# A fused decay-attention and Fourier-mixing kernel: the first batch's decay rates loaded two chunks at a time by token pairs, their running sums as two masked products, and a new stored order

## The chip, the cores and the metric

The kernel runs on one core of a Trainium2 chip. The metric is device time in microseconds (us) of one execution, from start to end, as the median of several runs. A profiled execution gives a trace besides: its span goes from the first to the last instruction. Engines are PE (matmul), ACT (ScalarE), DVE (VectorE), POOL (GpSimd) and SP, which here only issues transfers.

## The reference

Inputs are r, k, v, w of shape (4, 8, 768, 48): batch, head, token, channel. Every head carries a 48 x 48 state that each token's `w` decays:

```
cur   = outer(u * k[t], v[t])
y[t]  = r[t] @ (state + cur)
state = w[t][:, None] * state + outer(k[t], v[t])
```

The heads are then laid side by side, which gives x of shape (4, 768, 384), and a mixing block follows:

```
X   = fft(fft(x, axis=1), axis=2);  u = x + real(X)
un  = (u - mean(u)) / sqrt(var(u) + 1e-6)
out = u + relu(un @ w_ch1) @ w_ch2        # 384 -> 1536 -> 384
```

## The kernel before

**Attention.** The 768 tokens of a batch are six chunks of 128 tokens, one token to a partition; `attention(b, c)` writes the operations of one chunk. A chunk takes four loads (`load_one`, line 619), one each of w, k, r and v: 128 tokens x 8 heads x 48 channels. In memory the 48 fp32 channels of a token and head lie together, so each load moves 1024 runs of 192 B. The decays of a chunk become running sums of logarithms: ACT takes Ln of w into a bf16 buffer `LB` (line 793, shown under line 590, the helper's), and PE multiplies `LB` by a 0/1 mask over tokens, `MSK`, to get the sum over earlier tokens (line 795). A second mask, `NLE`, gives minus the sum up to and with the token itself (line 818, variant `sum_two`); in the variant `sum_add` DVE adds instead (line 832). `total` (lines 803 to 814) gives the sums over the whole chunk by five small products. Exponentials on ACT (lines 822 and 848) turn the sums into factors for r and k; DVE or POOL multiply them in, giving `RH` and `KH` (line 849; line 576, the helper's, `rkh<-in_k,e`). Both are transposed, either on PE with an eviction to `RKT` (lines 890 and 902) or by a transposing DMA from SP (line 880, `rkt<-rkh`). Then come scores (line 913), their masking on DVE (line 923), the state (lines 950 and 958) and the output (lines 975, 978 and 989). In the trace, `rkh` names both halves of one buffer, `ah` the masked scores and `e` the factors.

**Mixing.** `mix(b)` does the Fourier transforms as products with cosine and sine tables (lines 1054 to 1059 and 1098), the statistics (bn_stats, line 1155), the transposes of the normalised rows (on PE, line 1173, or by DMA, line 1180), the first layer (line 1205, with relu evictions at 1211 and 1213) and the second (line 1224, with outputs at 1233 and stores from SP at 1244). Before the first chunk the kernel makes its tables and masks from iotas (POOL, lines 630 to 636) by DVE arithmetic and two sine evaluations on ACT; ACT then loads a second function table (line 705), behind which the first Ln stands.

**What sets the order.** Every operation has a number. `ORDER` holds a list of numbers for each engine, written out by hand or by an earlier search; `schedule` only assigns PSUM banks along it, using estimates of durations. The engines run their lists in order and wait on semaphores. Where the program offers variants (`choose`) or engines, the list says which is used. Thirty-two products of constants (`warm`, line 1291), which nothing reads, and sixteen at the start (line 1257) keep PE occupied; their number is fixed. Input buffers hold seven chunks, `LB` three.

Of the kernel before, what the change touches and what calls it, by code (L numbers as in the profile page):

```python
# [20 lines left out]
PSUM_STATE, NE = 1, 16  # L21
# [44 lines left out]
    "act": (  # L66
# [384 lines left out]
def bass_rwkv6_finch__then__fnet_fourier_mix_kernel(  # L451
# [11 lines left out]
    DM = H * D  # L463
# [861 lines left out]
```

## Time and profile before

| | |
|---|---|
| Three runs, median | 183.09 us (182.51 to 184.56) |
| The profiled execution | 181.76 us |
| Its span, first to last instruction | 179.6 us |
| Around the span | 2.16 us |
| Granted PE clock, mean | 0.999 of full speed |

The profiled execution is 1.33 us below the median. A row of a group gives its busy time and the mean duration of one instruction; PE instructions overlap, so a product's mean duration is longer than the distance from its start to the next one's.

### The profile page before, as it was taken

Reading aid. Unit: us, or ns where it says so; the run is one execution under the profiler, and the core shown is the slowest. Engines: PE = TensorE matmul, PEld = TensorE weight load, DVE = VectorE, ACT = ScalarE, POOL = GpSimd, SP = SyncE. Lnnn points to the kernel's source line nnn. Section 1 sums busy time; section 2 is a strip of 40 time slices with the busy share of each in tenths; the row PEclk is TensorE's granted clock in tenths of the full one; section 3 lists DMA queues with packets and bytes.
Section 4 is the critical chain, followed back from the end, with each engine's and each line's share of the span. In section 5 each row is a group of like instructions: output and inputs, shape, how many; then the busy total and the mean of one; then the engine's idle time right before and its main releaser. Section 6 shows DMA issues by size and latency. Waiting matters only on the chain.

```text
span 179.6 us, 4554 instructions
## 1 busy us (share of the span) xinstructions
PE 172.1 (96%) x1704; PEld 113.7 (63%) x1704; DVE 159.5 (89%) x378; ACT 127.5 (71%) x306; POOL 107.7 (60%) x134
## 2 busy tenths in 40 slices
PE   4989899999999999999999999999989999999994
PEld 2456556766666667777666666766656766655663
DVE  7899899989999899999999999999999997971643
ACT  2899978679996578799999897989960775062200
POOL 2557969496705888499999964997862140500000
PEclk9999999999999999999999999999999999999999
DMA  6999999999999689999997999989972213034033
GB/s 118 217 210 225 183 206 193 203 216 179 162 205 204 145 173 224 199 211 217 202 239 137 224 182 240 235 155 197 245 71 56 74 47 65 1 60 141 0 131 131
DMA packets 117302, 29.28 MB, mean 163 GB/s; under 512 B 112545, under 2 KB 117282, under 8 KB 117282
## 3 DMA queue, kind: packets, MB, share of 16 engines
q1 hardware_dynamic: 115698, 26.65, 72.3%
q0 software_dynamic: 1584, 2.36, 7.9%
q8 instruction: 13, 0.21, 0.5%
q14 instruction: 7, 0.06, 0.1%
HBM read 23.59 MB, written 4.72 MB: 158 GB/s over the span
## 4 chain that ended last, share of the span: by engine, by line
PE 72%; DVE 13%; ACT 7%; POOL 3%; DMA 3%; issue 1%; POOLq 0%; DVEq 0%; ACTq 0%
PE bank L1205 23%; PE bank L1224 23%; PE bank L1098 4%; PE bank L1054 3%; PE bank L913 3%; DMA rkt<-rkh 3%; PE bank L890 2%; PE bank L795 2%; PE bank L978 2%; DVE bst L1155 2%; PE bank L975 1%; DVE uf L1128 1%; ACT rkt L599 1%; PE bank L950 1%; PE bank L818 1%
## 5 line engine op out<-in xcount | busy, mean ns | idle before, releaser
L1224 PE MATMUL bank<-w,ht 128*128 128x384 bf16 (+2 forms) x300 | 53.1, 320 | 0.0
L1205 PE MATMUL bank<-unt,w 128*128 128x384 bf16 x288 | 52.9, 326 | 0.0
L1213 ACT ACTIVATE ht<-bank 128x384 bf16<-128x384 f32 x70 | 31.0, 496 | 21.1 <-PE bank L1205 20.9
L1224 PEld LDWEIGHTS bank<-w,ht 128*128 128x128 bf16 x300 | 27.8, 98 | 15.6
L1205 PEld LDWEIGHTS bank<-unt,w 128*128 128x128 bf16 x288 | 26.6, 98 | 15.8 <-ACT ht L1213 0.2
L923 DVE TENSOR_TENSOR ah<-bank,msk 128x512 bf16<-128x512 f32 x44 | 28.7, 682 | 0.8 <-PE bank L913 0.6
L576 POOL TENSOR_TENSOR rk<-in_r,in_k 128x384 f32<-128x384 f32 x22 | 21.8, 999 | 1.9 <-issue 1.4
L576 POOL TENSOR_TENSOR rkh<-in_k,e 128x384 bf16<-128x384 f32 x18 | 18.0, 1003 | 6.7 <-ACT e L836 4.9
L576 POOL TENSOR_TENSOR rk<-rk,ub 128x384 f32<-128x384 f32 x20 | 19.8, 998 | 3.3 <-DVE rk L576 2.1
L576 POOL TENSOR_TENSOR vtd<-in_v,dc 128x384 f32<-128x384 f32 x20 | 16.4, 829 | 5.1 <-DVE sd L576 1.8
L599 ACT ACTIVATE rkt<-bank 128x512 bf16<-128x512 bf16 (+1 forms) x23 | 16.3, 713 | 4.3 <-PE bank L902 2.8
L1233 DVE SCALAR_TENSOR_TENSOR osb<-bank,rstd,uf 128x384 f32<-128x384 f32 (+2 forms) x24 | 14.3, 594 | 5.5 <-PE bank L1224 3.5
L1211 DVE TENSOR_SCALAR ht<-bank 128x384 bf16<-128x384 f32 x26 | 13.5, 548 | 5.4 <-PE bank L1205 5.2
L863 DVE TENSOR_REDUCE dc<-rk 128x8 f32<-128x384 f32 x24 | 12.7, 544 | 0.4 <-POOL rk L576 0.4
L848 ACT ACTIVATE bank<-bank 128x384 f32<-128x384 f32 x22 | 10.6, 488 | 3.0 <-PE bank L795 2.7
L590 ACT ACTIVATE lb<-in_w 128x384 bf16<-128x384 f32 x24 | 12.6, 528 | 0.1
L590 ACT ACTIVATE un<-uf,agg 128x384 bf16<-128x384 f32 x19 | 11.2, 618 | 1.5 <-DVE agg L1157 0.9
L849 DVE TENSOR_TENSOR rkh<-bank,in_r 128x384 bf16<-128x384 f32 x22 | 11.9, 547 | 0.2 <-ACT bank L848 0.2
L590 ACT ACTIVATE vb<-in_v 128x384 bf16<-128x384 f32 x22 | 11.5, 530 | 0.4 <-DMA in_v<-in_v_dram 0.3
L822 ACT ACTIVATE e<-bank 128x392 f32<-128x392 f32 (+1 forms) x18 | 8.8, 498 | 3.9 <-PE bank L809 2.5
L978 PE MATMUL bank<-vb,ah 128*128 128x48 bf16 x192 | 11.2, 183 | 0.0
L576 POOL TENSOR_TENSOR xf<-sd 128x384 bf16<-128x384 f32 (+1 forms) x7 | 6.9, 1002 | 6.1 <-DVE xf L576 3.9
(178 smaller groups left out, 365.1 us busy)
## 6 DMA issues: line engine op xcount, KB each, us to landing
in_r<-in_r_dram SPq DMA_DIRECT2D x24, 192.0 KB, 3.9
in_k<-in_k_dram SPq DMA_DIRECT2D x24, 192.0 KB, 3.8
in_w<-in_w_dram SPq DMA_DIRECT2D x24, 192.0 KB, 3.8
in_v<-in_v_dram SPq DMA_DIRECT2D x24, 192.0 KB, 3.8
out_dram<-osb SPq DMA_DIRECT2D x23, 192.0 KB, 2.9
w<-in_moe_w_ch_dram POOLq DMA_DIRECT2D x2, 576.0 KB, 7.9
w<-in_moe_w_ch_dram POOLq DMA_DIRECT2D x1, 1152.0 KB, 10.7
out_dram<-osb SPq DMA_DIRECT2D x1, 128.0 KB, 1.8
```

What stands on the lines that cost most here:

```text
L576: return lambda e: e.tensor_tensor(out=o, in0=a, in1=b, op=f)
L590: return lambda e: e.activation(o, a, f, **kw)
L599: {"act": lambda e: e.activation(o(), i(), ACTF.Copy), "dve": lambda e: e.tensor_copy(out=o(), in_=i())}, **kw)
L849: op("dve", v_1(DM), lambda e: e.tensor_tensor(out=rh[:, :, 0:D], in0=ps(tce)[:, 0:DM].rearrange("t (h d) -> t h d", d=D), in1=rt[:, :, :] ...
L863: op("dve", v_1(DM), lambda e: e.tensor_reduce(out=dc[:, :], in_=rku[:, :, :], axis=mybir.AxisListType.X, op=ALU.add), r=[("RK", i2)], w=[ ...
L923: masked[n].append(op("dve", v_1(512), lambda e: e.tensor_tensor(out=ah[:, x:H:2, :], in0=ps(bk)[:, :].rearrange("p (h t) -> p h t", t=128 ...
L978: ins = e.matmul(ps(ty)[:, D * h:D * h + D], ah[:, h, :], vb[:, h, :], start=first and not ype, stop=True, skip_group_check=True)
L1205: ins = e.matmul(ps(t)[:, 0:384], W1[:, m, 256 * (j // 2) + j % 2:256 * (j // 2) + 256:2], unt[:, :, m, :], start=(m == 0), stop=(m == NM ...
L1211: {"dve": lambda e, j=j, t=t, ht=ht: e.tensor_scalar(out=ht[:, j, :], in0=ps(t)[:, 0:384], scalar1=su, scalar2=0.0, op0=ALU.mult, op1=ALU. ...
L1213: "act": lambda e, j=j, t=t, ht=ht: e.activation(ht[:, j, :], ps(t)[:, 0:384], ACTF.Relu, scale=su)},
L1224: ins = e.matmul(ps(t)[:, 0:hi - lo], ht[:, j, 128 * x:128 * x + 128], W2[:, j, lo:hi], start=(j == 0), stop=(j == NJ - 1))
L1233: op("dve", v_1(hi - lo) + 64, lambda e: e.scalar_tensor_tensor(out=o[:, lo:hi], in0=ps(t)[:, 0:hi - lo], scalar=rstd[:, kb:kb + 1], in1=u ...
```

## The change

For batch 0 (`PAIRED = 1`), `load_pair` takes the place of two loads of w: one transfer for two chunks, in which partition p gets tokens 2p and 2p+1 of the 256. For each head the two tokens' channels lie together, so a run is 384 B. Ln runs twice, on the even and on the odd tokens, and the logarithms of a chunk are now spread over both `LB` buffers. Each of the two running sums is thus two accumulated products, with four masks of 128 x 256 (`PM`, in a buffer that the first mixing uses later). The chunk totals take four products more, against two half-indicators `HO` in place of a column of ones. All six chunks of batch 0 use `sum_two`, as they did before. DVE makes the masks and indicators at the start.

Besides this, row blocks of the other batches get a fourth variant (`add_sum`: the mean from an accumulated sum, the variance from an accumulating Square on ACT), four estimates of the scheduler differ, and the whole table `ORDER` is new. Of the table one line of each stands below.

```diff
-PSUM_STATE, NE = 1, 16
+PSUM_STATE, NE, PAIRED = 1, 16, 1
...
-        "7 2354 2355 2356 2357 2358 70 96 98 147 64 149 99 62 150 200 174 119 121 133 201 175 126 143 223 177 "
+        "7 2544 2545 2546 2547 2548 79 103 144 105 146 106 147 71 73 121 122 162 230 163 124 189 190 231 165 "
...
+    INW = sb("in_w", [NIN, H, D], FP32)
+    INB["w"] = [INW[:, i, :, :] for i in range(NIN)]
...
+    PM = UNT[0].rearrange("p a b t -> p (a b t)")[:, 0:1024].rearrange("p (x t) -> p x t", x=4)
...
     def load_one(b, c, n):
+        if n == "w" and b < PAIRED:
+            if c % 2 == 0:
+                load_pair(b, c)
+            return
...
+    def load_pair(b, c):
...
+        loads[b, c, "w"] = loads[b, c + 1, "w"] = op("sp", 750, lambda e: e.dma_start(
+            INW[:, i:i + 2, :, :].rearrange("p a h d -> p (a h d)").rearrange("p (h x) -> p h x", h=H),
+            w[b, :, c * CH:(c + 2) * CH, :].rearrange("h (p a) d -> p h (a d)", a=2)),
...
+        for x, (f0, f1, a1) in enumerate(((ALU.subtract, ALU.is_gt, 0.0), (ALU.subtract, ALU.is_gt, 1.0))):
+            dset(256, ts(PM[:, x, :], CI[:, 128:384], TC[:, 0:1], a1, f0, f1), r=["CI", "TC"], w=[("UNT", 0, x)])
+        dset(256, ts(PM[:, 2, :], CI[:, 128:384], TC[:, 0:1], -1.0, ALU.is_ge, ALU.mult), r=["CI", "TC"], w=[("UNT", 0, 2)])
+        dset(256, ts(PM[:, 3, :], CI[:, 128:384], TC[:, 0:1], -1.0, ALU.is_gt, ALU.mult), r=["CI", "TC"], w=["PM3"])
+        op("dve", 150, fill(PM[0:64, :, 128:256], 0.0), r=[("UNT", 0, 0), ("UNT", 0, 1), ("UNT", 0, 2), "PM3"],
+           w=["PMZ"])
+        op("dve", 60, ts(HO[:, 0, :], TC[:, 0:1].to_broadcast([128, 2]), 63.5, None, ALU.is_lt), r=["TC"], w=["HO0"])
+        op("dve", 60, ts(HO[:, 1, :], TC[:, 0:1].to_broadcast([128, 2]), 63.5, None, ALU.is_gt), r=["TC", "HO0"], w=["HO"])
...
+            def cum(t, m):
+                def f(e):
+                    for x in range(2):
+                        ins = e.matmul(ps(t)[:, 0:DM], PM[:, m + x, 128 * (c % 2):128 * (c % 2) + 128],
+                                       LB[l2[x]][:, :, 0:D], start=x == 0, stop=x == 1)
+                    return ins
...
+                    for x in ([LB[y] for y in l2] if paired else [L]):
+                        ins = e.matmul(ps(t)[:, DM + 2 * h:DM + 2 * h + 2],
+                                       x[:, 2 * h:2 * h + 2, :].rearrange("t h d -> t (h d)"),
+                                       HO[:, c % 2, :] if paired else ONE[:, :], start=False, stop=True,
+                                       skip_group_check=True)
...
+        if paired:
+            sum_two()
+        else:
+            g.choose(("sum", b, c), sum_two, sum_add, sum_key)
...
+                g.choose(("u", b, kb), add_bank, add_row, add_parts, add_sum)
```

Three places show what the new table does. The first is PE's list behind the start-up products, where the sums of chunks 0 and 1 stand; `lb0` and `lb1` are the logarithms, `msk` and `nle` the two masks, `unt0` the buffer that holds the new masks. Before:

```order
L656 MATMUL bank1<-osb0,vtd3 128x384
L795 MATMUL bank2<-lb0,msk 128x384
L818 MATMUL bank3<-lb0,nle 128x384
L795 MATMUL bank4<-lb1,msk 128x384
L749 MATMUL bank5<-ss,unt1 128x193
```

After:

```order
L686 MATMUL bank1<-osb0,vtd3 128x384
L837 MATMUL bank2<-lb0,unt0 128x384
L837 MATMUL bank2<-lb1,unt0 128x384
L837 MATMUL bank3<-lb0,unt0 128x384
L837 MATMUL bank3<-lb1,unt0 128x384
L837 MATMUL bank4<-lb0,unt0 128x384
L837 MATMUL bank4<-lb1,unt0 128x384
L837 MATMUL bank5<-lb0,unt0 128x384
L837 MATMUL bank5<-lb1,unt0 128x384
L856 MATMUL bank4<-pb,idw 128x8
```

Before, three products use one Ln each; after, eight products in a row, of which each bank's second needs the second Ln.

The second place is the head of DVE's list, up to the three instructions `uf<-osb,tc,ht` on which the sines wait. Before:

```order
L587 MEMSET bhpi 128x1
L580 TENSOR_SCALAR tn<-tc 128x3
L581 TENSOR_SCALAR pb<-tc 128x4
L581 TENSOR_SCALAR ht1<-osb2,tn 128x194
L587 MEMSET w1 128x384
L587 MEMSET vtd3 1x128
L587 MEMSET lb0 128x256
L581 TENSOR_SCALAR ht1<-osb2,tn 128x194 x2
L580 TENSOR_SCALAR idw<-osb1 128x384
L581 TENSOR_SCALAR ht1<-ht1 128x582
L584 SCALAR_TENSOR_TENSOR uf1<-osb2,tc,ht1 128x194 x3
```

After:

```order
L588 TENSOR_SCALAR ht1<-osb2,tn 128x194
L594 MEMSET w1 128x384
L588 TENSOR_SCALAR unt0<-osb1,tc 128x256
L588 TENSOR_SCALAR ht1<-osb2,tn 128x194
L594 MEMSET bhpi 128x1
L588 TENSOR_SCALAR ht1<-osb2,tn 128x194
L594 MEMSET rkh2 128x8x8
L588 TENSOR_SCALAR ht1<-ht1 128x582
L594 MEMSET vtd3 1x128
L588 TENSOR_SCALAR nle<-osb1 128x128
L591 SCALAR_TENSOR_TENSOR uf1<-osb2,tc,ht1 128x194
```

The identity (`idw`) has moved behind the three; one of the four new masks (`unt0`), `nle` and small fills have come ahead of them. On POOL the iotas now run in the order token index as integer, `osb1`, `tc`, `osb2`; before, `tc` and `osb2` came first.

The third place is SP's list at the last chunks' transposes, `rkt<-rkh`. Before:

```order
L622 DMA in_v1<-in_v_dram 128x8x48
L1244 DMA out_0_dram<-osb2 128x384
L1244 DMA out_0_dram<-osb0 128x384
L1244 DMA out_0_dram<-osb1 128x384
L880 DMA_TRANSPOSE rkt3<-rkh3 128x8x128
L880 DMA_TRANSPOSE rkt2<-rkh2 128x8x128
```

After:

```order
L633 DMA in_v1<-in_v_dram 128x8x48
L1324 DMA out_0_dram<-osb1 128x384
L633 DMA in_v2<-in_v_dram 128x8x48
L939 DMA_TRANSPOSE rkt2<-rkh2 128x8x128
L939 DMA_TRANSPOSE rkt3<-rkh3 128x8x128
L1324 DMA out_0_dram<-osb0 128x384
```

The three stores that stood right ahead of the two transposes are spread: one stands two places ahead, and one behind them.

More of the change, by code (lines that the diff above doesn't have):

```diff
@@ L299, in schedule @@
                 sw_t = a + o.xfer
+                a -= 200
                 sw.append((a, sw_t))
@@ L484, in bass_rwkv6_finch__then__fnet_fourier_mix_kernel @@
     NT = 4
-    INB = {n: [sb("in_%s%d" % (n, i), [H, D], FP32) for i in range(NIN)] for n in "wkrv"}
+    INW = sb("in_w", [NIN, H, D], FP32)
+    INB = {n: [sb("in_%s%d" % (n, i), [H, D], FP32) for i in range(NIN)] for n in "krv"}
+    INB["w"] = [INW[:, i, :, :] for i in range(NIN)]
     UB = sb("ub", [H, D], FP32)
@@ L508, in bass_rwkv6_finch__then__fnet_fourier_mix_kernel @@
     RSTD = [sb("rstd%d" % i, [NC], FP32) for i in range(2)]
+    MS = [sb("ms%d" % i, [NC, 3], FP32) for i in range(2)]
+    MCO = sb("mco", [2], FP32)
     UN = [sb("un%d" % i, [3, DM], BF16) for i in range(2)]
@@ L623, in load_one @@
                                                 src[n][b, :, c * CH:(c + 1) * CH, :].rearrange("h t d -> t h d")),
-               w=[("in", n, i)], sem="in_%s%d" % (n, i), xfer=985)
+               w=[("in", n, i)], sem="in_%s%d" % (n, i), xfer=998)
         loads[b, c, n] = o
+        g.ctx = was
+    def load_pair(b, c):
+        was, g.ctx = g.ctx, ("load", b, c, "w")
+        i = (b * NC + c) % NIN
+        loads[b, c, "w"] = loads[b, c + 1, "w"] = op("sp", 750, lambda e: e.dma_start(
+            INW[:, i:i + 2, :, :].rearrange("p a h d -> p (a h d)").rearrange("p (h x) -> p h x", h=H),
+            w[b, :, c * CH:(c + 2) * CH, :].rearrange("h (p a) d -> p h (a d)", a=2)),
+            w=[("in", "w", i), ("in", "w", i + 1)], sem="in_w%d" % i, xfer=1400)
         g.ctx = was
@@ L792, in attention @@
         xb = X[b % 2]
-        op("act", a_sb(DM), act(L[:, :, 0:D], wt[:, :, :], ACTF.Ln), r=[("in", "w", i3), "LOGEXP"], w=[("LB", i2)])
         tce = g.tile("a")
-        o = op("pe", mm(DM), lambda e: e.matmul(ps(tce)[:, 0:DM], MSK[:, :], L[:, :, 0:D]),
-               r=["MSK", ("LB", i2)], w=[tce])
+        paired = b < PAIRED
+        if paired:
+            c0 = c - c % 2
+            l2 = [(b * NC + c0 + x) % NB for x in range(2)]
+            if c == c0:
+                wp = INW[:, i3:i3 + 2, :, :].rearrange("p a h d -> p (a h d)").rearrange("p (h a d) -> p h a d", h=H, a=2)
+                for x in range(2):
+                    op("act", a_sb(DM), act(LB[l2[x]][:, :, 0:D], wp[:, :, x, :], ACTF.Ln),
+                       r=[("in", "w", i3), ("in", "w", i3 + 1), "LOGEXP"], w=[("LB", l2[x])])
+            def cum(t, m):
+                def f(e):
+                    for x in range(2):
+                        ins = e.matmul(ps(t)[:, 0:DM], PM[:, m + x, 128 * (c % 2):128 * (c % 2) + 128],
+                                       LB[l2[x]][:, :, 0:D], start=x == 0, stop=x == 1)
+                    return ins
+                return op("pe", mm(DM, 2), f, r=["PMZ", "PM3"] + [("UNT", 0, x) for x in range(3)]
+                          + [("LB", x) for x in l2], w=[t])
+            o = cum(tce, 0)
+        else:
+            op("act", a_sb(DM), act(L[:, :, 0:D], wt[:, :, :], ACTF.Ln), r=[("in", "w", i3), "LOGEXP"], w=[("LB", i2)])
+            o = op("pe", mm(DM), lambda e: e.matmul(ps(tce)[:, 0:DM], MSK[:, :], L[:, :, 0:D]),
+                   r=["MSK", ("LB", i2)], w=[tce])
         if n >= 2:
@@ L808, in tot @@
                 for h in range(HP):
-                    ins = e.matmul(ps(t)[:, DM + 2 * h:DM + 2 * h + 2],
-                                   L[:, 2 * h:2 * h + 2, :].rearrange("t h d -> t (h d)"), ONE[:, :], start=False,
-                                   stop=True, skip_group_check=True)
+                    for x in ([LB[y] for y in l2] if paired else [L]):
[3 more added lines that the diff above has]
+                                       skip_group_check=True)
                 return ins
             if not last:
-                op("pe", mm(1, 5), tot, r=["ONE", "IDB", "PB0", "PB", ("LB", i2)], w=[t])
+                op("pe", mm(1, 9 if paired else 5), tot, r=["HO0", "HO", "IDB", "PB0", "PB"] + [("LB", y) for y in l2]
+                   if paired else ["ONE", "IDB", "PB0", "PB", ("LB", i2)], w=[t])
         def sum_two():
             tci = g.tile("a")
-            op("pe", mm(DM), lambda e: e.matmul(ps(tci)[:, 0:DM], NLE[:, :], L[:, :, 0:D]),
-               r=["NLE", ("LB", i2)], w=[tci])
+            if paired:
+                cum(tci, 2)
+            else:
+                op("pe", mm(DM), lambda e: e.matmul(ps(tci)[:, 0:DM], NLE[:, :], L[:, :, 0:D]),
+                   r=["NLE", ("LB", i2)], w=[tci])
             total(tci)
@@ L844, in sum_key @@
             decays([("E2", i2)])
-        g.choose(("sum", b, c), sum_two, sum_add, sum_key)
+        if paired:
+            sum_two()
+        else:
+            g.choose(("sum", b, c), sum_two, sum_add, sum_key)
         def rh_bank():
@@ L1130, in add_bank @@
                        r=[t, ("X", i, kb)], w=[("UF", i, kb)])
+                    stats()
                 def add_row(kb=kb, t=t):
```

45 lines of the change are left out of this document (32 added, 13 removed), and 136 rows, old and new, of the table ORDER.

## Prediction

> **What bounds the kernel now.** I read the page first, then a table by stage, the chain of waits in order of time, the groups by form, and single stretches of the timeline.
>
> ```profile
> span 179.6 us, 4554 instructions
> PE 172.1 (96%) x1704; PEld 113.7 (63%) x1704; DVE 159.5 (89%) x378; ACT 127.5 (71%) x306; POOL 107.7 (60%) x134
> PE 72%; DVE 13%; ACT 7%; POOL 3%; DMA 3%; issue 1%; POOLq 0%; DVEq 0%; ACTq 0%
> ```
>
> PE is busy for 96% of the span, and the chain that ended last is PE for 72%. The next rows are stretches of the span: length, then busy time and count of PE, PEld, DVE, ACT and POOL, the granted clock, DMA share and GB/s.
>
> ```profile
> 0.00:5.00 5.00, 2.73 (x9) 1.34 (x10) 3.95 (x16) 1.47 (x2) 1.24 (x8) 1.00 0.67 130
> 5.00:10.00 5.00, 4.78 (x24) 2.10 (x21) 4.28 (x24) 4.74 (x8) 2.47 (x6) 1.00 1.07 214
> 10.00:15.00 5.00, 4.16 (x57) 2.98 (x56) 4.89 (x12) 4.68 (x11) 3.00 (x4) 1.00 1.08 213
> 15.00:20.00 5.00, 4.74 (x72) 3.23 (x73) 4.74 (x10) 4.92 (x12) 4.73 (x6) 1.00 1.01 197
> 20.00:25.00 5.00, 4.55 (x52) 2.60 (x50) 4.64 (x10) 4.14 (x11) 4.49 (x7) 1.00 1.05 205
> 28.00:133.20 105.20, 104.52 (x1132) 70.82 (x1131) 101.36 (x230) 90.12 (x219) 81.52 (x92) 1.00 1.00 195
> 133.20:179.60 46.40, 43.80 (x327) 28.70 (x327) 32.63 (x76) 14.55 (x41) 8.36 (x12) 1.00 0.25 71
> 170.00:179.60 9.60, 7.04 (x56) 4.77 (x53) 4.18 (x9) 0.49 (x1) 0.00 (x0) 0.99 0.35 123
> ```
>
> There are three stages. Up to 28 us, batch 0's attention: DVE works 14.27 of the 15 us from 10 to 25, ACT 13.74, and the DMA engines are full (shares over 1.00). From 28 to 133.2, everything at once: PE idles 0.68 us of 105.2. From 133.2, matmul work with nothing in its way. The chain of waits (start, length, what) names who holds each stage.
>
> ```profile
> 3.63 1.09 DVE uf L584 x3
> 4.81 0.70 ACT ss L590
> 6.40 1.29 ACT L705
> 7.77 0.53 ACT lb L590
> 8.35 0.34 PE bank L795
> 57.85 1.95 PE bank L1224 x12
> 128.14 0.47 DVE rkh L849
> 128.63 4.57 DMA rkt<-rkh
> 133.24 0.40 PE bank L913 x8
> ```
>
> The start is DVE, sines, the second ACT table, Ln. The only DMA in the chain, its 3%, is the last transpose: PE reaches the last chunk's scores at 133.24 when that lands. Twelve 384-column products take 1.95 us, 0.1625 each from start to start.
>
> **The change part by part.** First the counts, from the two lists of order. PE gets 24 of the new sum products, 6 `MSK` products fewer and 7 `NLE` products fewer (six for batch 0, one elsewhere): 11 more of 384 columns, 11 x 0.1625 = 1.79 us. It gets 20 two-column products more, and one fp32 product of `vtd` fewer (two records).
>
> ```profile
> 98.36 0.24 PE L809 MATMUL bank<-one,lb 128*128 128x2 bf16 x4
> 98.46 0.81 PE L1224 MATMUL bank<-w,ht 128*128 128x384 bf16 x4
> 17.37 0.86 PE L998 MATMUL bank<-vtd,ht 128*128 128x384 f32 x2
> 18.07 0.33 PE L795 MATMUL bank<-lb,msk 128*128 128x384 bf16 x1
> ```
>
> Four of the small ones hold the next product off by 0.10 us, so 20 cost 0.50; the fp32 product holds PE 0.70 (from 17.37 to 18.07). PE's work rises by 1.79 + 0.50 - 0.70 = 1.6 us. All of the rise lies in batch 0, where PE is waited for by others but itself waits; and a lone product is recorded busy for 0.33 us although the next could start after 0.16, so the second of a pair fits into the first one's tail. On the path it costs its 0.16 once per sum.
>
> Second, the **start**. DVE gets four masks of 128 x 256, a zeroing, two indicators and two one-column constants.
>
> ```profile
> L580 DVE TENSOR_SCALAR idw<-osb 128x384 bf16<-128x384 f32 x1 | 0.3, 341 | 0.0
> L580 DVE TENSOR_SCALAR msk<-osb 128x128 bf16<-128x128 f32 x1 | 0.2, 221 | 0.0
> 0.84 0.15 POOL L630 IOTA tc<- 128x6 f32 x1 [0.40 <-POOLq L1310]
> 1.88 0.46 POOL L634 IOTA osb<- 128x384 f32 x1 [0.46 <-DVE ht L581]
> ```
>
> A mask lies between the 128-column one (221 ns) and the 384-column one (341): 4 x 0.28 = 1.1, and 0.5 for the five small ones (each between nothing and 0.22): 1.6 us, bounds 0.9 to 2.5. DVE idled 1.05 + 0.72 us in the first 10, partly before it had anything to do, so about 0.8 is covered. POOL now makes the 0.46 us iota ahead of `tc`, from which DVE's chain to the sines starts: the first Ln comes about 0.5 later, at 8.3. The first sum needs both Lns, 0.41 more, and two products: its result moves from 8.35 + 0.34 to about 9.7. That is less bad than it looks, since DVE uses it late.
>
> ```profile
> 10.53 1.01 DVE L849 TENSOR_TENSOR rkh<-bank,in_r 128x384 bf16<-128x384 f32 x2
> 25.65 0.54 DVE L576 TENSOR_TENSOR rkh<-in_k,e 128x384 bf16<-128x384 f32 x1
> 26.11 0.54 DVE L576 TENSOR_TENSOR rk<-in_r,in_k 128x384 f32<-128x384 f32 x1
> L923 DVE TENSOR_TENSOR ah<-bank,msk 128x512 bf16<-128x512 f32 x44 | 28.7, 682 | 0.8 <-PE bank L913 0.6
> ```
>
> Following DVE's new list with these spacings (0.47 for 384 columns, as from 25.65 to 26.11; 0.60 for a mask of scores, its 682 ns less the same overlap of 0.08), I get the first `rkh<-bank` at 10.75 against 10.53. Between there and the last r and k factors of batch 0 the list has 25 costly instructions before (six `rkh<-bank`, four `rkh<-in_k`, eight `ah`, four `st`, three `dc`, ...), 14.1 us in a stretch of 15.58; after, 15.0 us, since a product, a cast and a copy came to DVE. Its end then lies between 10.75 + 15.0 = 25.8 (no waits left) and 27.2 (the old 1.4 us of waits kept), against 26.11: -0.4 to +1.1. I take +0.3, nearer the lower end, because the loads of w now come first and all sums are ready sooner.
>
> Third, the **loads**. With 192-B runs the engines move 213 GB/s at a share of 1.08 (10 to 15 us): 12.3 GB/s an engine, 15.6 ns a run. At the end, where nearly only stores of 1536-B runs move, 123 GB/s at 0.35: 22 GB/s, 70 ns a run. A straight line between gives 23.4 ns for 384 B. A load is 64 runs an engine, 1.0 us; two cost 2.0, a pair 1.5. Three pairs save 1.5 us; bounds 0 (price by bytes) and 3.0 (price by runs).
>
> ```profile
> 16.35 1.83 SPq L622 DMA_DIRECT2D in_w<-in_w_dram  x1
> 19.74 1.02 SPq L622 DMA_DIRECT2D in_k<-in_k_dram  x1
> 21.96 0.57 ACT L590 ACTIVATE lb<-in_w 128x384 bf16<-128x384 f32 x1
> DMA to landing us min/median/max: 3.4/3.8/10.7
> ```
>
> On the path I cost this at nothing: the last w of batch 0 is issued at 16.35, lands some 3.8 later, and Ln takes it at 21.96, when ACT gets there. DVE and ACT, 95% and 92% busy, are the cover; without it up to 1.5 us would come through. The new list also spends the saving. The last k of batch 0 is issued at 19.74 and lands near 23.6, behind 21 loads; after, 17 single loads and three pairs stand ahead of it, worth 23 loads without a saving and 21.5 with it, so it lands no earlier.
>
> Fourth, the **long middle**. From batch 0's last scores to the last chunk's scores, PE's products priced by their spacings sum to 102.6 us before and 102.8 after; behind the last scores to 43.9 in both. So the end follows the middle, +0.2. The 105.2 us hold 2.6 us of waits by that price (0.68 by the records). One is 0.51 at 133.24.
>
> ```profile
> PE bank L913 <- DMA rkt<-rkh: 0.5, 1, 0.5
> ```
>
> There the last transpose took 4.57 us behind three stores, two of which are moved away: -0.5. DVE, which the chain names ahead of it, has by the same prices 2.8 us less to do between batch 0's last factor and the last `rkh`, what the start got in excess. I let a third of the other 2.1 us of waits go, -0.7; ACT (3.6 us more) and POOL (2 us more) have 15 and 24 us to spare there.
>
> The sum: +0.3 + 0.2 - 0.5 - 0.7 = -0.7 us. Span 178.9, the profiled execution (2.16 around it) 181.1 instead of 181.76; that execution lay 1.33 below the median, so the median is 183.09 - 0.7 = 182.4.
>
> **The rivals.** *Earlier decay rates pull the whole start.* All waits of DVE vanish in batch 0 (25.6 instead of 26.11, -0.5), and the waits of the middle but 0.8 go too (-1.8), with +0.2 of work: -2.1, 181.0. For it: the DMA engines are full from 5 us on, and w's loads come first now. Against: no load stands in the chain.
>
> *DVE's new work at the start is paid in full.* The 1.6 us of constants find no cover, the start of DVE's chain is 0.5 later, and the waits stay (+1.1 for the list), while the middle gains nothing, less 0.5 for the transpose, which the moved stores still give: +0.2 + 1.6 + 0.5 + 1.1 - 0.5 = +2.9, 186.0 at the worst; about +2.3, 185.4, with 0.6 of cover. It decides from the point at which the last factors of batch 0 leave DVE after 28.2. For it: DVE is 95% busy there and all later work queues behind it. Against: 1.8 us of idle in its first 10.
>
> *The pair costs as much as two loads.* No DMA saving; the last k, two loads later than before, would land at about 25.5 instead of 23.6 us, just when DVE wants it: about +0.3 on the forecast, 182.7. The Trainium skill, "DMA: Bandwidth & Descriptors", section "Specifications", gives 512 B as the least transfer for line rate, below which the engine reads, modifies and writes; by that rule 384 B would stay at the slow rate, and this rival would hold. No run here yet shows a 384-B run.
>
> **How the numbers follow.** About 1%, 1.83 us, is what a measurement of this kernel can tell from no change. The forecast has 0.47, the pair without a saving 0.08: both within 1%, 0.55 together. The first rival has 0.25 (faster by over 1% from 181.26 down), the second 0.20. The predicted time is the forecast's, 182.4. Its own range, from the bounds of DVE's list (-0.4 to +1.1) and of the waits (none to all of the 2.1), is 181.0 to 184.0. The range of 8 in 10 reaches into both rivals: 180.7 to 185.0.
>
> **What would show it.** In the changed kernel's profile: the first Ln near 8.3 and the first `rkh<-bank` near 10.75; the last factors of batch 0 between 25.8 and 27.2; the paired load moving 384 KB in about 1.5 us; PE's busy time up by 1 to 2 us with less idle before 28 us; the last scores no longer behind a transpose, near 132.5; 46.4 us from there to the end. If the last scores come after 135, DVE's start was the price; if before 131.4, the loads or the lighter middle were worth more than I give them. If the tail is not 46 us, the prediction rests on the wrong stage.

## The result, and the profile after

Over 19 runs of each kernel on the same chips the changed kernel takes 183.45 us in the median (182.77 to 186.05), the kernel before 182.84 (181.53 to 187.15). The ratio is 1.0056 with a 95% interval of 1.003 to 1.0082: about 1.0 us slower, where the forecast had 0.7 us faster. That is less than the 1% which the forecast took as the least that could be told, but the interval leaves out no change and the predicted gain alike.

The profiled execution of the changed kernel took 183.45 us, just its median; that of the kernel before had lain 1.1 us under its own. So about 1.1 us of what lies between the two profiled executions (1.7 us in time, 1.9 in span) is the luck of a single profile, and a difference between two stages below needs a second profile before it counts. The head of the page after:

```profile
span 181.5 us, 4619 instructions
PE 172.9 (95%) x1733; PEld 114.9 (63%) x1733; DVE 158.2 (87%) x386; ACT 133.0 (73%) x314; POOL 110.6 (61%) x135
PE 65%; DVE 14%; SPq 7%; DMA 5%; issue 3%; POOL 2%; ACT 1%; DVEq 0%; POOLq 0%
```

PE is busy for 0.8 us more, DVE for 1.3 less. The change is in the third line: SP's queue (7%) and DMA (5%) now stand in the chain that ended last, where DMA had 3%, all of it one transpose, and SP nothing. Loads have come onto the path. Two places of the chain, in order of time, say which:

```profile
11.71 4.70 DMA in_v<-in_v_dram
16.43 0.53 ACT vb L597
...
92.16 5.15 DMA in_k<-in_k_dram
97.44 1.02 POOL rk L583
```

The stages end where the scores of the last chunk of batch 0 and of the last chunks of batch 3 begin. These are PE's rows for them:

```profile
28.94 0.40 PE L972 MATMUL bank<-rkt 48*128 48x128 bf16 x8
134.99 0.62 PE L972 MATMUL bank<-rkt 48*128 48x128 bf16 x16
```

Before, they began at 27.99 and 133.24, the latter for the last chunk alone. After, the last two chunks share one row of sixteen; the last chunk's own eight begin about 0.2 us into it (sixteen take 0.62 us, eight 0.40). In this pair of profiles the start is 0.95 us longer, the middle 106.05 us in place of 105.25, and the tail 46.5 in place of 46.4. The wait for a transpose ahead of the last scores is gone, as forecast: the second row carries no idle time. But the middle is longer all the same. Between these two rows PE is busy for 104.80 us (before, 104.53) and idle for 1.25 (before, 0.72, of which 0.51 was the wait for the transpose). Nearly all of the idle time now stands in two rows:

```profile
101.51 0.40 PE L961 MATMUL bank<-idw,rkh 128*128 128x128 bf16 x4 [0.48 <-POOL rkh L583]
108.02 0.32 PE L874 MATMUL bank<-lb,nle 128*128 128x384 bf16 x1 [0.67 <-DVE rkh L908]
```

What made POOL and DVE late is seen in four rows of the stretch around 100 us, on POOL, on SP and on DVE:

```profile
97.44 1.01 POOL L583 TENSOR_TENSOR rk<-in_r,in_k 128x384 f32<-128x384 f32 x1 [0.90 <-DMA in_k<-in_k_dram]
101.12 2.27 SPq L633 DMA_DIRECT2D in_r<-in_r_dram  x2
105.05 0.55 DVE L908 TENSOR_TENSOR rkh<-bank,in_r 128x384 bf16<-128x384 f32 x1
107.32 0.56 DVE L908 TENSOR_TENSOR rkh<-bank,in_r 128x384 bf16<-128x384 f32 x1 [1.72 <-ACT ht L1293]
```

POOL waits 0.90 us for a load of k, and DVE 1.72 us, it says, for a relu eviction of ACT. For the two loads of r in the second row (issued at 101.12 and 101.91) the view of the tile gives this time from issue to landing:

```profile
DMA to landing us min/median/max: 4.3/4.8/5.3
```

The second is the one of 5.3 and landed at 107.2. That is 0.1 us ahead of DVE's start at 107.32, and by the order of DVE's list this is the product that reads it: r of batch 3's chunk 1. The eviction named was not what ended the wait. SP's two lists, put beside the times of issue, show that both loads have moved: k of batch 3's chunk 0, for which POOL waits, was issued at 81.0 us before and is at 92.16 now, r of its chunk 1 at 90.9 and now 101.91. Before, they landed 12.7 and 10.3 us ahead of their first use.

### The profile page after: what moved, and what is told of

Same layout as the page of the kernel before. It is cut to its first block, busy times and chain, and to the rows that moved or that the text cites. A ratio compares the mean times of both kernels' runs of the same rounds, so it can differ in the third digit from the quotient of the medians.

```text
span 181.5 us, 4619 instructions
## 1 busy us (share of the span) xinstructions
PE 172.9 (95%) x1733; PEld 114.9 (63%) x1733; DVE 158.2 (87%) x386; ACT 133.0 (73%) x314; POOL 110.6 (61%) x135
## 4 chain that ended last, share of the span: by engine, by line
PE 65%; DVE 14%; SPq 7%; DMA 5%; issue 3%; POOL 2%; ACT 1%; DVEq 0%; POOLq 0%
PE bank L1285 22%; PE bank L1304 20%; SPq L633 4%; PE bank L1157 4%; DVE ah L982 3%; DMA in_k<-in_k_dram 3%; PE bank L972 3%; DMA in_v<-in_v_dram 3%; PE bank L1113 2%; SPq L642 2%; PE bank L1371 2%; PE bank L961 2%; DVE rkh L908 2%; DVE uf L1200 2%; PE bank L1037 1%
## 5 line engine op out<-in xcount | busy, mean ns | idle before, releaser
L1293 ACT ACTIVATE ht<-bank 128x384 bf16<-128x384 f32 x71 | 32.6, 497 | 13.3 <-PE bank L1285 13.0
L1285 PEld LDWEIGHTS bank<-unt,w 128*128 128x128 bf16 x288 | 26.9, 98 | 16.0 <-DVE unt L607 0.2
L982 DVE TENSOR_TENSOR ah<-bank,msk 128x512 bf16<-128x512 f32 x41 | 26.5, 682 | 0.6 <-PE bank L972 0.6
L583 POOL TENSOR_TENSOR vtd<-in_v,dc 128x384 f32<-128x384 f32 x23 | 19.0, 830 | 7.0 <-DVE rk L583 2.7
L583 POOL TENSOR_TENSOR rk<-rk,ub 128x384 f32<-128x384 f32 x21 | 20.9, 1003 | 2.1 <-DVE rkh L583 1.0
L583 POOL TENSOR_TENSOR rk<-in_r,in_k 128x384 f32<-128x384 f32 x19 | 19.0, 1005 | 3.0 <-DMA in_k<-in_k_dram 1.8
L606 ACT ACTIVATE rkt<-bank 128x512 bf16<-128x512 bf16 (+1 forms) x19 | 14.7, 779 | 3.8 <-PE bank L961 2.8
L583 POOL TENSOR_TENSOR uf<-uf,xf 128x191 f32<-128x191 f32 x7 | 4.1, 591 | 15.0 <-DVE uf L1220 13.9
L583 POOL TENSOR_TENSOR xf<-sd 128x382 bf16<-128x382 f32 (+1 forms) x9 | 8.9, 1001 | 6.7 <-DVE xf L583 2.5
L583 POOL TENSOR_TENSOR rkh<-in_k,e 128x384 bf16<-128x384 f32 x12 | 12.0, 1002 | 0.0
L1048 DVE TENSOR_TENSOR x<-bank,vtd 128x384 f32<-128x384 f32 x19 | 10.4, 551 | 0.9 <-PE bank L1037 0.9
```

The source lines that it names most:

```text
L583: return lambda e: e.tensor_tensor(out=o, in0=a, in1=b, op=f)
L606: {"act": lambda e: e.activation(o(), i(), ACTF.Copy), "dve": lambda e: e.tensor_copy(out=o(), in_=i())}, **kw)
L982: masked[n].append(op("dve", v_1(512), lambda e: e.tensor_tensor(out=ah[:, x:H:2, :], in0=ps(bk)[:, :].rearrange("p (h t) -> p h t", t=128 ...
L1285: ins = e.matmul(ps(t)[:, 0:384], W1[:, m, 256 * (j // 2) + j % 2:256 * (j // 2) + 256:2], unt[:, :, m, :], start=(m == 0), stop=(m == NM ...
L1293: "act": lambda e, j=j, t=t, ht=ht: e.activation(ht[:, j, :], ps(t)[:, 0:384], ACTF.Relu, scale=su)},
```

## The experiments

Each kernel is compared with runs of the kernel before on its own chip. The theories: A, the paired form costs the time (more products, sums that need two Ln, constants on DVE); B, the new order costs it, by loads that now land just when they are wanted, at the start or in the middle.

### The pair and the order taken apart

**new_order_single**: the new order, without pairs.

```diff
-PSUM_STATE, NE, PAIRED = 1, 16, 1
+PSUM_STATE, NE, PAIRED = 1, 16, 0
 # SP, at each pair's place
-L642 DMA in_w<-in_w_dram 128x8x96
+L633 DMA in_w<-in_w_dram 128x8x48 x2
```

> The changed kernel's stored order on every engine, but each chunk of batch 0 has its own load of decay rates (two single loads stand where the pair stood), its own Ln and the old masks; the row masks and the half vectors aren't made. Theory A, the paired form costs the time (11 more products of 384 columns, sums that need two Ln, 1.6 us of constants): without it the time falls to the kernel before or under it, ratio to before 0.995 to 1.000, and the 6th scores stand near 28.0 us as before. Theory B, the new order costs it (loads of v and k that land just as they are needed, products moved to VectorE): the ratio stays at 1.004 to 1.008; and if the pair's shorter load also mattered in that order, it is up to 1.012, since three pairs of 1.5 us become six loads of 1.0.

Measured: 186.57 us, ratio 1.0196 (1.0147 to 1.0244), more than either theory had. PE's rows at the third chunk, and a table by stretch (length, busy time of PE, PEld, DVE, ACT and POOL, granted clock, DMA share, GB/s):

```profile
19.44 1.03 PE L953 MATMUL bank<-idw,rkh 128*128 128x128 bf16 x8 [1.46 <-DVE rkh L900]
32.17 0.40 PE L964 MATMUL bank<-rkt 48*128 48x128 bf16 x8
```

```profile
13.70:18.35 4.65, 3.38 (x54) 2.18 (x51) 3.77 (x9) 3.57 (x7) 3.63 (x6) 1.00 1.05 202
18.35:22.90 4.55, 3.46 (x21) 2.30 (x21) 3.02 (x7) 2.27 (x5) 3.88 (x6) 0.53 0.91 177
22.90:27.50 4.60, 4.07 (x49) 2.72 (x49) 3.26 (x6) 3.73 (x9) 3.37 (x4) 0.72 1.04 201
```

The loss is all at the start: the 6th scores come at 32.17, and 104.7 us lie from there to the last, fewer than in either kernel. But a part of it is not the loads: around an idle of 1.46 us the granted clock falls to 0.53, so PE's work in the next stretches takes up to twice as long. All six executions of this kernel have a mean clock of 0.97 to 0.98. Nothing here supports theory A, since taking the pairs out of this order makes nothing faster; but how much slower the loads alone would make it the run doesn't show, so the size of the pair's own worth has to come from the next kernel.

**runs192**: pairs, each issued as two transfers of 192-byte runs.

```diff
-            INW[...].rearrange("p (h x) -> p h x", h=H),
-            w[...].rearrange("h (p a) d -> p h (a d)", a=2)),
+        for x in range(2):
+                pair[:, :, x, :],
+                w[...].rearrange("h (p a) d -> p h a d", a=2)[:, :, x, :]),
```

> The changed kernel with each paired load issued as two transfers, one for each token parity, in runs of 192 bytes in place of 384; order, sums and everything else are the changed kernel's. If pairs cost as two single loads anyway, or if batch 0's loads are hidden: the same as the changed kernel, ratio to before 1.004 to 1.008. If the longer runs save 0.5 us a pair and the loads of v2, k3 and the third pair end the waits of the start: those land 0.5, 1.0 and 1.5 us later, 6th scores near 29.5 to 30.2, ratio 1.008 to 1.013.

Measured: 185.60 us, ratio 1.0168 (1.0113 to 1.0223), so 1.1% or 2.0 us over the changed kernel. Not all of that is the loads: in the three executions with a clock of 1.00, the profiled one among them, the kernel took 184.64 to 185.09 us, in the three with 0.99 it took 186.10 to 187.23. Where the clock held, it is some 1.0% over the kernel before, so some 0.5%, or 0.9 us, over the changed kernel; that rests on three executions. ACT's copy of v of chunk 2 and the 6th scores:

```profile
18.73 0.52 ACT L597 ACTIVATE vb<-in_v 128x384 bf16<-128x384 f32 x1 [1.37 <-DMA in_v<-in_v_dram]
30.61 0.40 PE L974 MATMUL bank<-rkt 48*128 48x128 bf16 x8
```

The copy starts 2.3 us later than in the changed kernel and the scores 1.7. The longer runs save time, and in this order a part of it lies on the path. What a run of 384 bytes costs follows from the packets of 5 to 15 us, of the kernel before and of the changed one:

```profile
DMA packets 11273, 2.13 MB, mean 213 GB/s; under 512 B 11272, under 2 KB 11273, under 8 KB 11273
q1 hardware_dynamic: 11273, 2.13, 107.8%
```

```profile
DMA packets 9157, 2.33 MB, mean 233 GB/s; under 512 B 9156, under 2 KB 9156, under 8 KB 9156
q1 hardware_dynamic: 9156, 2.32, 105.0%
```

Before: 16 engines x 10 us x 1.078 over 11273 packets is 15.3 ns for 192 bytes. After, 9156 packets with 2.32 MB are some 2950 of 384 bytes and 6200 of 192; 168 us less 6200 x 15.3 leaves 24.7 ns for the long ones. A pair takes 64 x 24.7 = 1.6 us of every engine, two loads 1.96.

**new_start** and **new_rest**: the two orders joined at the end of batch 0's attention, either way round.

```diff
 # new_start: paired; new_rest: not paired
-ORDER = {...}
+ORDER = {...}   # one kernel's rows for tables, constants, batch 0's loads, attention and folds; the other's for the rest, merged by time
```

> Paired, with the changed kernel's order for the tables, the constants, batch 0's loads, attention and folds, and the order of the kernel before for all that follows (the two lists merged by time). Theory A and also theory B with its cost in the start: 6th scores near 28.9 us, ratio 1.004 to 1.008 in all. Theory B with half of its cost in the rest (the wait near 92 to 107 us): 6th scores near 28.9 and the rest as in the kernel before, last scores 0.9 after the old place, ratio 1.002 to 1.006, and no wait of the kind at 92 to 107 us. The seam between the two lists may cost some tenths of a us itself.

> Unpaired, the kernel before's order up to the end of batch 0's attention and folds, and the changed kernel's order for all that follows (merged by time). Theory A: ratio 0.997 to 1.001, because the paired form is gone. Theory B with half of its cost in the rest: 6th scores near 28.0 as before, last scores near 134.1 against 133.2, ratio 1.003 to 1.006, and POOL's product waits for a load of k near 92 to 97 us again. If the rest of the new order is the better one by itself, as the forecast had it (the last transpose off the path, 0.5, and VectorE with less to do, 0.7): ratio 0.992 to 0.996.

Measured: 1.0601 (1.0559 to 1.0642) and 1.0203 (1.0145 to 1.0261), with the 6th scores at 35.2 and 31.4 us. Both lose at the seam, before the stage that they were made to test; in new_start PE works 1.57 of the 4.8 us up to 28.8, and the clock is at 0.50 behind that. They tell nothing of A or B. These two orders, planned as wholes, couldn't be cut and joined.

### The start

**vb_behind**, **pair3_behind** and **kh5_pool** take away one suspect each, **all_three** all of them.

```diff
 # vb_behind: ACT
-L597 ACTIVATE vb<-in_v 128x384
 L907 ACTIVATE bank<-bank 128x384
 L878 ACTIVATE e_0<-bank 128x392
 L907 ACTIVATE bank<-bank 128x384
+L597 ACTIVATE vb<-in_v 128x384
 # pair3_behind: SP (and the first Ln of the pair next to the second)
-L642 DMA in_w<-in_w_dram 128x8x96
 L633 DMA in_v<-in_v_dram 128x8x48
 L633 DMA in_r<-in_r_dram 128x8x48
 L633 DMA in_k<-in_k_dram 128x8x48
+L642 DMA in_w<-in_w_dram 128x8x96
 # kh5_pool: DVE, then POOL
-L583 TENSOR_TENSOR rkh<-in_k,e_2 128x8x48
+L583 TENSOR_TENSOR rkh<-in_k,e_2 128x8x48
```

> The changed kernel with one row moved on ScalarE: the copy of v of chunk 2, which waits for its load until 16.43 us, stands behind the two exps of chunks 2 and 3 on a bank and the exp between them, in place of ahead of them. If the late load of v is what the start loses (it holds the exp for chunk 2's r factor back from 16.1 to 16.96): 3rd scores near 19.2 in place of 19.8, 6th near 28.3 in place of 28.9, ratio to before 1.001 to 1.003. If VectorE is full from 17 to 28 us and sets the end of the start: at most its 0.4 of waiting comes back, 6th scores 28.6 to 28.9, ratio 1.003 to 1.008.

> The changed kernel with the third paired load (chunks 4 and 5) moved behind v2, r3 and k3 in SP's order, and the first of its two Ln moved on ScalarE to stand beside the second. v2 should land near 15.0 in place of 16.4 and k3 near 17.2 in place of 18.7. If the start waits for these loads, because a pair asks for an odd chunk's rates earlier than they are needed: 6th scores 28.0 to 28.4, ratio 1.000 to 1.003. If VectorE's work sets the end of the start: 6th scores 28.6 to 28.9, ratio 1.003 to 1.008. If the sums of chunks 4 and 5 now come late (their Ln ends near 21.4 either way): 6th scores after 29.2.

> The changed kernel with the k factor of chunk 5 on POOL, behind its second product with the bonus for chunk 4, in place of VectorE. POOL is idle there for 0.96 us and the product takes it 1.0. If VectorE's load in 17 to 28 us (products that stood on POOL before, and its gaps beside POOL's products) sets the end of the start: VectorE is 1.0 us earlier from 26.0 on, chunk 5's r factor ends near 26.0 in place of 26.9, 6th scores 28.3 to 28.7, ratio 1.001 to 1.004. If the loads set it: no change at the 6th scores, 28.9, ratio 1.004 to 1.008; if POOL becomes late with the product: 29.2 and above.

> The three moves of the other kernels of this call together on the changed kernel. If each gives what its own theory says they add up to about 1 us before the 6th scores: 6th scores near 27.9 and ratio 0.997 to 1.001, so the paired form would then cost nothing against the kernel before. If only one of the two theories holds: 6th scores near 28.4, ratio 1.000 to 1.004.

| | ratio | interval | 6th scores, us |
|---|---|---|---|
| vb_behind | 1.0038 | 0.9992 to 1.0085 | 28.60 |
| pair3_behind | 1.0143 | 1.0106 to 1.0181 | 28.79 |
| kh5_pool | 1.0074 | 1.0035 to 1.0114 | 28.97 |
| all_three | 1.0047 | 1.0018 to 1.0076 | 28.70 |

Nothing moves the 6th scores by more than 0.35 us, by one profile each: no one of these three suspects alone sets the start. In pair3_behind v arrives in time, but the middle is worse, and again at the same two instructions, POOL's and DVE's:

```profile
99.70 1.00 POOL L583 TENSOR_TENSOR rk<-in_r,in_k 128x384 f32<-128x384 f32 x1 [1.36 <-DMA in_k<-in_k_dram]
109.88 0.56 DVE L908 TENSOR_TENSOR rkh<-bank,in_r 128x384 bf16<-128x384 f32 x1 [2.03 <-DMA in_r<-in_r_dram]
```

Here the profile names the load of r itself.

**no_row_masks**: without the four masks; one fill with zeros stands at the first mask's place, and every product still runs.

```diff
-        for x, (f0, f1, a1) in enumerate(...):
-            dset(256, ts(PM[:, x, :], ...
...
-        op("dve", 150, fill(PM[0:64, :, 128:256], 0.0), ...
+        op("dve", 300, fill(PM[:, :, :], 0.0), ...
```

> The changed kernel with the four row masks and their zeroed half left out (one fill with zeros in place of five instructions), so the running sums of batch 0 aren't computed; every product on them still runs. VectorE has about 1.0 us less to do before 9 us. If the constants' time is paid at the start (a term that the forecast put near 0.3 in all): first scores 13.0 to 13.7 in place of 14.0 and 6th scores 28.0 to 28.6. If other work of VectorE's hid it: first scores 13.9 to 14.1, 6th 28.7 to 29.0, ratio as the changed kernel's, 1.003 to 1.008.

Measured: ratio 1.0065 (1.0023 to 1.0107). PE's rows for the first and the 6th scores:

```profile
14.25 0.40 PE L967 MATMUL bank<-rkt 48*128 48x128 bf16 x8 [0.34 <-ACT rkt L606]
29.14 0.40 PE L967 MATMUL bank<-rkt 48*128 48x128 bf16 x8
```

Neither is earlier than with the masks (13.98 and 28.94). The edit takes 1.5 us off DVE (four of 0.31 and a fill of 0.27) and puts 0.48 on it, and the 0.48 stand ahead of the sines, where the first mask took 0.23: the first Ln comes at 8.32 in place of 8.04. From the first Ln to the first scores it is 5.93 us, with the masks 5.94. So the three masks and the fill that stand behind the sines are hidden; the first mask, ahead of them, this run doesn't take off the path.

### The middle: two loads

**loads_early** moves the two late loads forward; **loads_early_vb** also moves ACT's copies of v of chunks 2 and 3 in batch 0; **k30_early** and **r31_early** move one of the loads each.

```diff
 # SP: k of batch 3's chunk 0 (loads_early, loads_early_vb, k30_early)
-L633 DMA in_w<-in_w_dram 128x8x48
+L633 DMA in_k<-in_k_dram 128x8x48
...
-L633 DMA in_k<-in_k_dram 128x8x48
-L633 DMA in_w<-in_w_dram 128x8x48
+L633 DMA in_w<-in_w_dram 128x8x48 x2
 # SP: r of its chunk 1 (loads_early, loads_early_vb, r31_early)
 L1260 DMA_TRANSPOSE unt<-un 128x9x128
+L633 DMA in_r<-in_r_dram 128x8x48
 L633 DMA in_k<-in_k_dram 128x8x48
 L1324 DMA out_dram<-osb 128x384
 L633 DMA in_v<-in_v_dram 128x8x48
-L633 DMA in_r<-in_r_dram 128x8x48 x3
+L633 DMA in_r<-in_r_dram 128x8x48 x2
```

> The changed kernel with only SP's order in the middle altered: the load of k of batch 3's chunk 0 changes places with the load of w of its chunk 2 (issued 92.2 and 81.5 us, needed near 93.7 and 107.9), and the load of r of its chunk 1 (issued 101.9, landed 107.2 when VectorE began its product with it at 107.32) stands ahead of the load of k of that chunk. If the new order's late places for these two loads cost the middle its time: no wait of POOL for k near 97 us, no 1.7 us of idle on VectorE at 105.6, last scores 0.7 to 1.4 earlier (133.7 to 134.4), ratio to before 0.997 to 1.001. If the middle is bound elsewhere and these waits are covered: last scores 134.8 to 135.3, ratio 1.003 to 1.008.

> The same with ScalarE's copies of v of chunks 2 and 3 of batch 0 moved behind the exps that they stood ahead of, since each waited for its load (16.43 and about 23.2 us). If the start gains the 0.3 us that moving the first of them gave, or a little more from the second, and the middle what the loads give: 6th scores 28.3 to 28.6, ratio 0.994 to 0.999, which would be a version under both kernels. If the start's gain is lost again in the middle, as it was when the copy of chunk 2 was moved alone: the ratio of the kernel with the loads only.

> The changed kernel with only the first of the two moves: the load of k of batch 3's chunk 0 in the place of the load of w of its chunk 2, and the other way round; the load of r of chunk 1 stays late (issued 101.9, landed 107.2). If both loads cost time one after the other: POOL's 0.9 us wait near 97 is gone, VectorE's wait of 1.7 us for r at 105.6 stays, and the ratio to before lies between, 1.002 to 1.004. If r alone is what the end feels, since everything behind k waits for r again: ratio 1.004 to 1.007, as the changed kernel. If k alone was it: 0.998 to 1.002, as with both moves.

> The changed kernel with only the second of the two moves: the load of r of batch 3's chunk 1 ahead of the load of k of that chunk on SP, so that it lands near 102.5 in place of 107.2; the load of k of chunk 0 stays late (landed 97.3). If r alone is what the end feels: no idle of 1.7 us on VectorE at 105.6, PE's stalls in 105 to 110 us near 0.1 to 0.3 in place of 0.9, ratio to before 0.998 to 1.002, as with both moves. If both loads must come early, since the wait for k only hides behind that for r: POOL's product still waits for k to 97.4, PE stalls in 100 to 105, ratio 1.002 to 1.005.

| | ratio | interval |
|---|---|---|
| changed kernel | 1.0056 | 1.003 to 1.0082 |
| k30_early | 1.0086 | 1.005 to 1.0122 |
| r31_early | 1.0044 | 1.0014 to 1.0075 |
| loads_early | 1.0002 | 0.9969 to 1.0035 |
| loads_early_vb | 0.9978 | 0.9942 to 1.0014 |

With both loads early the ratio shows no loss (its interval and that of the changed kernel just overlap, at 1.003 to 1.0035). The two instructions, in loads_early:

```profile
96.24 1.01 POOL L583 TENSOR_TENSOR rk<-in_r,in_k 128x384 f32<-128x384 f32 x1
104.27 1.07 DVE L908 TENSOR_TENSOR rkh<-bank,in_r 128x384 bf16<-128x384 f32 x2
```

Neither waits any more, and DVE's two products stand next to each other. The pairs are all still there, so this speaks against theory A: the paired form costs nothing that the ratio shows. (The profiled execution took 183.94 us, above its median of 183.18, and its last scores came at 135.50: PE waited 0.85 and 0.83 us for two later transposes.) In k30_early POOL doesn't wait, but DVE's wait for r grew, and in r31_early it is the other way round. First k30_early, then r31_early:

```profile
108.92 0.56 DVE L908 TENSOR_TENSOR rkh<-bank,in_r 128x384 bf16<-128x384 f32 x1 [2.67 <-DMA in_r<-in_r_dram]
```

```profile
97.34 1.00 POOL L583 TENSOR_TENSOR rk<-in_r,in_k 128x384 f32<-128x384 f32 x1 [0.73 <-DMA in_k<-in_k_dram]
104.94 1.15 DVE L908 TENSOR_TENSOR rkh<-bank,in_r 128x384 bf16<-128x384 f32 x2
```

Work that is freed from the first wait runs into the second, so k alone gives nothing, and r alone little that can be told from the changed kernel. By the ratios alone both are needed, though the intervals of r31_early and loads_early overlap. In loads_early_vb the two rows of scores and the table of the middle are:

```profile
28.71 0.40 PE L972 MATMUL bank<-rkt 48*128 48x128 bf16 x8
133.59 0.62 PE L972 MATMUL bank<-rkt 48*128 48x128 bf16 x16
```

```profile
28.70:133.60 104.90, 104.83 (x1130) 70.90 (x1129) 99.95 (x226) 91.56 (x227) 82.98 (x92) 1.00 0.99 195
```

The middle is 104.9 us, and PE is busy for all but 0.07. One profile is little to go by: in that of r31_early, with k still late, the middle is 104.96, and in that of loads_early 106.83. The ratio of loads_early_vb says more. Its interval lies wholly below the changed kernel's, so this version is the faster of the two; that it is faster than the kernel before its interval doesn't show.

**before_r31_late**: the kernel before, with one load put late and nothing else of the change.

```diff
-L622 DMA in_r<-in_r_dram 128x8x48 x2
+L622 DMA in_r<-in_r_dram 128x8x48
...
 L622 DMA in_w<-in_w_dram 128x8x48
+L622 DMA in_r<-in_r_dram 128x8x48
 L880 DMA_TRANSPOSE rkt<-rkh 128x8x128 x2
```

> The kernel before with one load moved: r of batch 3's chunk 1 (issued 90.9, landed 94.8; VectorE's product with it runs at 105.1) now stands behind the load of w of chunk 2, issued near 102.5 and landing near 107 to 108. Nothing else of the changed kernel is in it. If the place of this load is what the changed kernel loses: VectorE waits some 2 to 3 us for it near 105, last scores 134.0 to 135.5 in place of 133.2, ratio 1.003 to 1.010. If the kernel before has room there (its work behind that product needed later): ratio 0.999 to 1.002.

Measured: 184.30 us against 181.62, ratio 1.0149 (1.0108 to 1.0191). Its rows of DVE and of PE:

```profile
108.43 0.56 DVE L849 TENSOR_TENSOR rkh<-bank,in_r 128x384 bf16<-128x384 f32 x1 [2.49 <-DMA in_r<-in_r_dram]
```

```profile
29.05 0.40 PE L913 MATMUL bank<-rkt 48*128 48x128 bf16 x8
137.28 0.67 PE L913 MATMUL bank<-rkt 48*128 48x128 bf16 x16
```

One load, landing some 2.5 us after its use was due, makes the kernel before slower by 2.7 us, more than the whole change does. (The profiled execution took 186.09 us, above the median: its granted clock is 0.94 between 90 and 120 us, while the other five executions have 1.00 in the mean.)

The PE rows hold something else: up to here the program is the kernel before, word for word, and its 6th scores come at 29.05, in the first profile at 27.99. The sixteen start-up products tell why. Here are those of the kernel before in its first profile, then in before_r31_late:

```profile
2.27 4.22 PE L1257 MATMUL bank<-w 128*128 128x384 bf16 x16 [2.27 <-DVE w L587]
2.26 5.30 PE L1257 MATMUL bank<-w 128*128 128x384 bf16 x16 [2.26 <-DVE w L587]
```

The same products take 1.08 us more, all that follows on PE is later, and the start of the kernel before carries the delay to its end. Profiles of the changed kernel and its variants have both lengths too, but it takes the delay up on the way: with 4.36 us of start-up products its 6th scores come at 28.94, and in loads_early, k30_early and r31_early, which have its start, with 5.19 to 5.30 at 28.67 to 29.00. So like with like, the start is 0.95 us longer after short start-up products and 0.05 to 0.4 shorter after long ones. How often each occurs in executions without a profile isn't known, and of the kernel before's start there is one profile of each kind.

## Why the prediction was wrong, point by point

**The long middle: this step failed.** It had 105.25 + 0.2 - 0.5 - 0.7, so 104.2; it came to 106.05. The +0.2 for PE's work was right (104.80 us busy in place of 104.53), and so was the -0.5, since the transpose no longer ends a wait. What failed is the -0.7, the waits that were to go. It took DVE's smaller load as a gain, and to that end I had read SP's new list only at batch 0's loads and at the last transposes. Between them k of batch 3's chunk 0 and r of its chunk 1 are each issued some 11 us later. They land when POOL and DVE are already waiting (0.90 and 1.72 us), and behind these two PE waits 0.48 and 0.67: 1.15 us of waits came where 0.7 were to go. With both loads in early places the ratio falls by 0.0054, about 1.0 us, nearly the whole of the loss. Whether the gain that the step spoke of is there once they are isn't shown: the best profile has a middle of 104.9 us (loads_early_vb), 0.35 under the kernel before and 0.7 over the forecast, and its ratio doesn't tell it from the kernel before.

**The start: right in mechanism, its size open.** The first Ln came at 8.04 (forecast 8.3), the first r factor from a bank at 10.17 (10.75). For the last factor, the row of DVE is:

```profile
26.37 0.55 DVE L908 TENSOR_TENSOR rkh<-bank,in_r 128x384 bf16<-128x384 f32 x1
```

It ends at 26.9, inside 25.8 to 27.2 and 0.5 behind the 26.4 that I took. The 6th scores came 0.95 later than in the first profile, where the sum had +0.3; the start-up products, which the prediction doesn't price, decide how much of that there is. Most of the constants were covered, as no_row_masks shows, and the last factors left DVE well before the 28.2 that was to decide for it, so the rival by which DVE's new work is paid in full is refuted. My marker for it misled: the last scores did come at 135.0, 1.75 us later than before, but 0.95 of that was there at the 6th scores, and the rest is the middle. A mark at the end of a long stage doesn't say which part of it was long; the 6th scores would have.

**The loads: the price right, its place wrong.** A pair takes 1.6 us of the engines by the packets (1.5 forecast, 24.7 ns a run where I had 23.4). The rival that it costs as much as two loads is refuted, and with it my reading of the rule that was to carry it. The Trainium skill, "DMA: Bandwidth & Descriptors", section "Specifications", names 512 B as the least for line rate. That doesn't put all shorter runs at one slow rate: here 384-byte runs move 384 / 24.7 = 15.5 GB/s an engine against 12.5 for 192. They are still below the 22 GB/s that the prediction read from the stores of 1536-byte runs, so nothing here speaks against what the Trainium skill states, and no run here has runs of 512 bytes. "On the path nothing" was wrong for the new order: it counts on the saving, and without it loses some 0.5% where the clock holds, and 1.1% in the median of all executions.

**PE's work and the tail.** The count came as forecast (29 records more, 11 + 20 - 2), and so did the tail, 46.5 us behind the last scores. The busy time rose by 0.8 us, half of the 1.6 and outside the 1 to 2 that were to show it, and there was not less idle before 28 us but more: PE is busy for 23.17 us up to there in place of 23.76.

**Still open**: why moving the third pair back costs the middle another 0.9% by itself and not in all_three, which has the same move; what the start costs in the mean over short and long start-up products; and whether the last 0.2% of the better version against the kernel before is real.

## What to carry to other kernels

When a stored order changes, read the list of the load queue to its end and compare, for each load, its landing with its first use: a load with 10 us to spare is free to move, and the same load moved 11 us costs more than the change it came with. In a kernel whose DMA engines are full for two thirds of its span, the order of the loads is as much a resource as the engines' time. And a shorter transfer is not hidden or exposed by itself: the order decides, and here the order made for it spent it. Before two profiles are compared stage by stage, compare what both kernels do first; here the start-up products alone set two profiles of one kernel's start 1.08 us apart.

## What the runs showed of the hardware

- **Short idles came with a halved PE clock, but not each time.** In new_order_single PE idled 1.46 us before 19.44, after shorter gaps, and the granted clock was 0.53 in the stretch of 4.55 us around and behind it and 0.72 in the one after; all six executions have a mean of 0.97 to 0.98. In the profile of runs192 PE idled more there (busy for 2.40 of the 5 us from 15 to 20, with an idle of 1.22) and the clock stayed at 1.00, while three of its six executions have a mean of 0.99. The Trainium skill, "TensorE: Matmul & The Clock Gate", section "Part 1: The HAM clock gate (the "warmup" mystery)", gives an idle window of about 3.4 us as the condition; this idle was less than half of that. What decides is not settled by these runs.
- **The same start-up products vary from execution to execution.** Sixteen products of 384 columns took 4.22 us in the profile of the kernel before and 5.30 in that of before_r31_late, which has the same start, where sixteen at the spacing of later products (0.1625 us) would take 2.6.
- **The releaser that the profile names was wrong where a load landed close.** The same wait of DVE is put down to ACT's eviction in the changed kernel (1.72 us) and to the load of r in three others (2.03, 2.67, 2.49). The time of issue plus the tile's time to landing settled it.
